# One core, packed attention and two feed-forward layers: loads over all partitions, a shared layout of e and v, other slots for raw weights, and a table that shifts the planner's order

## The chip, the cores and the metric

The kernel runs on one core of one Trainium2 chip. The metric is the device time of one launch in microseconds (us). A profile is one more execution, taken with the hardware profiler. Six queues matter: TensorE (PE; its weight loads are shown apart as PEld), VectorE (DVE), ScalarE (ACT), GpSimd (POOL), and the queue of SyncE (SP), which issues nearly all DMAs; ACT issues the others. Each engine takes its instructions strictly in program order and waits on semaphores for data from the others.

## The reference

```
p_packed = softmax(scale * p @ k.T) @ v              # per batch and head: 32 packed rows, 576 tokens, width 64
attn     = softmax(scale * q @ p_packed.T) @ p_packed
x = attn.transpose(0, 2, 1, 3).reshape(4608, 512)
h = x @ w_in                                          # 512 -> 1024
solu = h * softmax(h)
ln = (solu - mean(solu)) / sqrt(var(solu) + 1e-6) * g_ln
y = ln @ w_out                                        # 1024 -> 512
out = relu(y @ w2_in) ** 2 @ w2_out                   # 512 -> 2048 -> 512
```

There are 8 batches, 8 heads and 4608 = 8 x 576 tokens. The weights arrive as double-precision words, two 32-bit words for each value, and are put together on the engines.

## The kernel before

**Stages.** A batch's attention is done in two halves. `pack` computes p_packed: DVE transposes k (kT), q (qT) and p (pT) in blocks of 32 (L601, L637), PE makes the scores s (L615), DVE takes their maxima (mx), ACT their exponentials e, PE transposes e (pt, L680), ACT copies the result out (eT), PE multiplies it by v (ppp, L690), and DVE scales it into pp and pd (L694, L696). PE transposes those two (ptp) and ACT copies them out as ppf and ppq. `unpack` makes the second scores and their softmax (tiles a, m, d, aT), and G = p_packed @ w_in (pg, L626; ACT and DVE write it as a high part and a rest). Then h comes as aT times G, in 36 tiles of 128 tokens (`h_tile`): products ph, on DVE the maximum nm (L815) and the product e (L823), on ACT two passes, PE transposes (ptv), and ACT and DVE write the tile v (a high part by ACT and the rest by DVE, each in two pieces of 512 a tile). Two tiles make a y stage (`y_stage`): 96 products py (three for each pair of operands, since each operand is a high part and a rest), 18 such stages in all, written to y_dram. Beside that run the decodings of the weights: w_in (4 chunks of 1024 columns, `load_w_in`), w_out (4 chunks, `load_w_out`), and 16 pieces of w2_in (`prepare`, tiles w2raw, wx, wh), whose results go to z_dram and are loaded again (zi) for the last two stages: z (products px, pw, pz) and o (px, pa).

**The order.** No engine's order is written by hand. Each operation is recorded with an engine, an estimate of its time and an urgency. `Plan.order` plays the program through by these estimates: of the operations that are ready on an engine, the one with the least urgency goes first. `emit` repeats this with urgencies worked back from the end, keeps the best, and then records the instructions in the order found. A gate is a mark that holds back the first transposes (kT, qT) of a batch in this order until a given maximum nm is recorded; it puts no other wait on the chip than those two operations have anyway.

**Slots.** A tile waits until the tile that held its slot is done with. The raw words of w_out (wraw) sit in the two slots v00 and v01, where chunks 0 and 1 of w_in's raw words lie first. So the first two loads of w_out cannot be issued before chunks 0 and 1 of w_in are decoded, and SP, which issues in order, holds everything behind them back too. The raw tiles of k and q have three slots, those of v two.

**Decoding.** One chunk costs ACT one pass (L525) and DVE five; with `sign == DVE` two of DVE's put the sign in (L528, L529), with `sign == ACT` two ACT passes (L532, L534) take the place of the first of them. Before, w_in goes by DVE and w_out by ACT.

Of the kernel before, what the change touches and what calls it, by code (L numbers as in the profile page):

```python
# [94 lines left out]
class Plan:  # L95
# [241 lines left out]
    def emit(self, passes):  # L337
        order = self.order()
        best, kept = max(self.ends), None
        for _ in range(passes):  # L340
            self.backward()
            urgencies = [o.urgency for o in self.ops]
            order = self.order()
            if max(self.ends) < best:
                best, kept = max(self.ends), urgencies
        if kept:
            for o, u in zip(self.ops, kept):
                o.urgency = u
# [9 lines left out]
def kernel(  # L358
# [37 lines left out]
    ST = 256  # L396
    AB, RAW, TMP, VR, ET = 4, 3, 4, 2, 2
    LEAD = 2
    QA, GA, HA, TR, UN = 15.37, 149.84, 60.66, -52.41, -15.5
    WD, WDS, WIS = 101.7, 198.675, 19.564  # L400
    SIN, SOUT = DVE, ACT
    GX = 1
# [71 lines left out]

    RATES = {256: 205.0, 512: 303.0, 1024: 341.0, 1536: 372.0, 2304: 300.0, 3072: 378.0, 4096: 410.0, 8192: 400.0}
# [90 lines left out]
    def load_w_out(at, d):  # L566

        raw = wo_v.tile([P, C1 * P, 2], I32, "wraw", tag=f"v0{d % 2}")
        dma(-1995.0 + 0.1 * d, lambda: raw().rearrange("p (c d) w -> p c d w", c=C1),
            lambda: w_out_bits[:, 2 * d * P:2 * (d + 1) * P].rearrange("(c p) (d w) -> p c d w", p=P, w=2), P * C1 * P * 8, w=[raw], run=1024)  # L570
        x = wo_v.tile([P, C1 * P], F32, "wx", tag=f"v1{d % 2}")
        decode(at, raw, C1 * P, x, SOUT, add=(DVE,))
        xv = lambda: x().rearrange("p (c d) -> p c d", c=C1)

        def gain():
            for c in range(C1):
                nc.scalar.mul(xv()[:, c], xv()[:, c], g_neg[:, c:c + 1])
# [7 lines left out]
    KC, KJ = 3 * T, 2 * 3  # L585
# [42 lines left out]
    def pack(at, b):  # L628
# [10 lines left out]
        mx = [ab.tile([P, 2], F32, f"mx{g}") for g in range(NG)]  # L639
        e1s = [ab.tile([P, S], F32, "e1", bufs=2) for _ in range(NG)]  # L640
        s1 = []
# [5 lines left out]

        vs = []
        for g in range(NG):
            vr = ab.tile([P, HG, KJ, D], F32, "vr", bufs=VR)  # L650
            dma(first(b, "v", at + 1), lambda vr=vr: vr()[:KC].rearrange("p e j d -> p e (j d)"), lambda g=g: v[b, g::NG].rearrange(
                "e (p j) d -> p e (j d)", j=KJ), HG * S * D * 4, w=[vr], run=1536)
            vs.append(vr)

# [3 lines left out]
        for g in range(NG):  # L658
# [13 lines left out]

            eT = ab.tile([P, KJ, P], F32, "eT", bufs=ET)
            for hf in range(2):
                pte = bank("pt")
                js = range(hf * KJ // 2, (hf + 1) * KJ // 2)

                def pt_tr(js=js, pte=pte, e1=e1):
                    for n, j in enumerate(js):
                        nc.tensor.transpose(pte()[:KC, n * P:(n + 1) * P], e1()[:, j::KJ], ident)  # L680
                plan.op(PE, 3 * 109, at + 7, pt_tr, r=[e1], w=[pte], claim=[eT])
                hi_op(at + 7, 3 * P, lambda hf=hf, eT=eT: eT()[:KC, hf * 3:(hf + 1) * 3],
                      lambda pte=pte: pte()[:KC, :3 * P].rearrange("p (j n) -> p j n", n=P), [pte], [eT])

            ppp = bank("ppp")

            def pp_mm(g=g, ppp=ppp, eT=eT):
                for j in range(KJ):
                    for e in range(HG):
                        nc.tensor.matmul(ppp()[32 * e:32 * e + 32, :D], eT()[:KC, j, 32 * e:32 * e + 32], vs[g]()[:KC, e, j],  # L690
                                         start=j == 0, stop=j == KJ - 1)
            plan.op(PE, KJ * 2 * 80 + 60, at + 10, pp_mm, r=[eT, vs[g]], w=[ppp], claim=[pp, pd])
            plan.ops[-1].tiled = True
            plan.op(DVE, c_dve(D) + 60, at + 12, lambda g=g, ppp=ppp, rs=rs: nc.vector.tensor_scalar(  # L694
                pp()[:, g], ppp()[:, :D], rs(), None, op0=ALU.mult), r=[ppp, rs], w=[pp])
# [221 lines left out]
    for b in range(B):  # L917
# [354 lines left out]
```

## Time and profile before

| What | us |
|---|---|
| Three timed runs: median (lowest, highest) | 1243.34 (1242.59, 1245.89) |
| The profiled execution: its own time | 1245.66 |
| Its span, first to last instruction | 1243.9 |
| PE busy | 1174.1 (94%) |
| DVE busy | 886.0 (71%) |
| ACT busy | 793.0 (64%) |
| POOL busy | 167.8 (13%) |

The profiled execution took 1.8 us more than its span, and 2.3 us more than the median of the timed runs. A busy PE is not PE at its peak: products overlap in the array, so a matmul's duration is longer than the distance from its start to the next one's. Where the engine runs without a gap, that distance is what counts.

### The profile page before, as it was taken

The page shows a single profiled execution, that of the slowest core. Times are in us where ns is not written, and L with a number is a line of the kernel's source. Part 1 is how long each engine was busy: PE and PEld are TensorE (multiplying, and loading weights), DVE is VectorE, ACT ScalarE, POOL GpSimd, SP SyncE. Part 2 cuts the span into 40 slices and gives each one's busy share as a digit, 9 for nine tenths or more (in the row PEclk, how much of TensorE's full clock was granted, in tenths as well). Part 3 has the DMA queues.
Part 4 walks back from the last instruction along what each step waited for, and adds up shares of the span by engine and source line. Part 5 has one row for each costly group of instructions (what it writes and reads, how often), then busy time and mean ns, then how long its engine had stood idle before and what let it go on. Part 6 is the DMA issues. An engine that isn't in the chain of part 4 may idle for free.

```text
span 1243.9 us, 25577 instructions
## 1 busy us (share of the span) xinstructions
PE 1174.1 (94%) x9684; PEld 1088.7 (88%) x9684; DVE 886.0 (71%) x1724; ACT 793.0 (64%) x1669; POOL 167.8 (13%) x225
## 2 busy tenths in 40 slices
PE   3289999999999999889999999999999999999998
PEld 2036776788989899879999999999999999999998
DVE  4799988976476645437675857573779787878885
ACT  3388757766667766538787878786645454545452
POOL 0012543434244333000000000000000000000000
PEclk9989999999999999999999999999999999999999
DMA  9964988622322322995857565746994535262601
GB/s 259 196 157 118 226 203 218 167 65 93 112 69 77 115 77 72 367 363 182 263 189 257 191 234 191 233 153 219 382 399 153 165 103 164 92 189 67 191 14 52
DMA packets 174012, 218.75 MB, mean 176 GB/s; under 512 B 18240, under 2 KB 140608, under 8 KB 173120
## 3 DMA queue, kind: packets, MB, share of 16 engines
q1 hardware_dynamic: 133472, 192.20, 49.8%
q10 hardware_dynamic: 40416, 24.91, 6.6%
q8 instruction: 76, 1.25, 0.4%
q14 instruction: 48, 0.39, 0.1%
HBM read 131.08 MB, written 85.98 MB: 175 GB/s over the span
## 4 chain that ended last, share of the span: by engine, by line
PE 83%; DMA 7%; DVE 6%; ACT 2%; issue 1%; SPq 1%; ACTq 0%; DVEq 0%
PE px L510 10%; PE px L512 10%; PE px L511 10%; PE ph L808 7%; PE py L510 5%; PE pa L512 5%; PE pa L511 5%; PE pa L510 5%; PE py L512 5%; PE py L511 5%; PE pz L512 3%; PE pz L510 3%; PE pz L511 3%; PE s L615 2%; PE ptv L852 2%; DMA zi<-z_dram 1%
## 5 line engine op out<-in xcount | busy, mean ns | idle before, releaser
L492 ACT CAST cb<-ga 128x384 fp32r<-128x384 f32 x336 | 167.9, 514 | 161.5 <-PE pa L512 70.5
L495 DVE TENSOR_TENSOR cb<-ga,cb 128x384 fp32r<-128x384 f32 x336 | 180.8, 555 | 57.7 <-ACT cb L492 56.4
L510 PE MATMUL py<-v,wo 128*128 128x256 f32 x576 | 167.6, 291 | 2.9 <-ACT v L492 1.4
L511 PE MATMUL py<-v,wo 128*128 128x256 f32 x576 | 163.5, 284 | 0.8 <-DVE v L495 0.8
L512 PE MATMUL py<-v,wo 128*128 128x256 f32 x576 | 163.4, 284 | 0.0
L510 PE MATMUL px<-oi,cb 128*128 128x256 f32 x504 | 142.2, 282 | 0.8 <-ACT gw L1084 0.8
L512 PE MATMUL px<-oi,cb 128*128 128x256 f32 x504 | 142.3, 282 | 0.0
L510 PE MATMUL pa<-oi,cb 128*128 128x256 f32 x504 | 142.0, 282 | 0.0
L512 PE MATMUL pa<-oi,cb 128*128 128x256 f32 x504 | 142.0, 282 | 0.0
L511 PE MATMUL px<-oi,cb 128*128 128x256 f32 x504 | 142.0, 282 | 0.0
L511 PE MATMUL pa<-oi,cb 128*128 128x256 f32 x504 | 142.0, 282 | 0.0
L512 PE MATMUL px<-y,zi 128*128 128x384 f32 x384 | 129.7, 338 | 1.1 <-DMA zi<-z_dram 1.1
L510 PE MATMUL px<-y,zi 128*128 128x384 f32 x384 | 129.4, 337 | 1.3 <-ACT gw L1053 1.3
L511 PE MATMUL px<-y,zi 128*128 128x384 f32 x384 | 129.3, 337 | 0.0
L510 PEld LDWEIGHTS py<-v,wo 128*128 128x128 f32 x576 | 110.7, 192 | 10.6 <-issue 3.6
L511 PEld LDWEIGHTS py<-v,wo 128*128 128x128 f32 x576 | 110.7, 192 | 2.2 <-DVE v L495 1.2
L512 PEld LDWEIGHTS py<-v,wo 128*128 128x128 f32 x576 | 110.6, 192 | 0.0
L1057 DVE TENSOR_TENSOR gw<-pz,gw 128x384 f32<-128x384 f32 x96 | 53.3, 555 | 77.1 <-PE pz L512 58.0
L997 DVE TENSOR_TENSOR ga<-ga 128x384 f32<-128x384 f32 x192 | 100.5, 552 | 2.3 <-DMA ga<-g_dram 1.4
L510 PEld LDWEIGHTS px<-oi,cb 128*128 128x128 f32 x504 | 95.4, 189 | 1.0 <-ACT gw L1084 1.0
L512 PEld LDWEIGHTS px<-oi,cb 128*128 128x128 f32 x504 | 95.3, 189 | 0.1
L1065 ACT ACTIVATE gw<-gw 128x384 f32<-128x384 f32 x116 | 60.8, 524 | 54.3 <-DVE gw L1057 53.9
(142 smaller groups left out, 2941.1 us busy)
## 6 DMA issues: line engine op xcount, KB each, us to landing
g_dram<-gw SPq DMA_DIRECT2D x192, 192.0 KB, 2.6
ga<-g_dram SPq DMA_DIRECT2D x96, 384.0 KB, 4.1
zi<-z_dram SPq DMA_DIRECT2D x28, 512.0 KB, 8.7
oi<-o_dram SPq DMA_DIRECT2D x24, 512.0 KB, 9.5
kr<-in_k_dram SPq DMA_DIRECT2D x32, 288.0 KB, 5.5
qr<-in_q_dram SPq DMA_DIRECT2D x32, 288.0 KB, 6.1
vr<-in_v_dram SPq DMA_DIRECT2D x16, 576.0 KB, 7.4
y_dram<-ysb ACTq DMA_DIRECT2D x72, 128.0 KB, 2.0
```

The source lines that it names most:

```text
L492: plan.op(ACT, c_act(cols, sbuf=r[0].pool not in (psm, psh, pso)), at, lambda: nc.scalar.copy(out_(), in_()), r=r, w=w)
L495: plan.either(on(cols, *engines), at, lambda e: vec[e].tensor_tensor(out_(), in_(), hi_().bitcast(F32), op=ALU.subtract), r=r, w=w, port=i ...
L510: nc.tensor.matmul(ps, lh, rh, start=first, stop=False, skip_group_check=onto)
L511: nc.tensor.matmul(ps, lh, rl, start=False, stop=False, skip_group_check=onto)
L512: nc.tensor.matmul(ps, ll, rh, start=False, stop=last, skip_group_check=onto)
L615: nc.tensor.matmul(banks[u]()[32 * e:32 * e + 32, :SH].rearrange("p (m t) -> p m t", t=T), lhs(ps, e, f), ts[e // 2]()[ps, e % 2, :, f], s ...
L808: nc.tensor.matmul(ph()[:, fs], al[l]()[:, g], g_tiles[b, g]()[:, r, fs], start=ends[0] and g == 0 and t == 0, stop=ends[1] and g == NG - ...
L852: nc.tensor.transpose(pt()[:, c * P:(c + 1) * P], e()[:, (4 * t + c) * P:(4 * t + c + 1) * P], ident)
L997: plan.op(DVE, c_dve(cols), at, lambda: nc.vector.tensor_tensor(out_(), in0(), in1(), op=op), r=r, w=w, port=True)
L1057: plan.op(DVE, c_dve(HN), when(p, SN), lambda: nc.vector.tensor_tensor(t(), ps()[:, :HN], t(), op=ALU.add), r=[t, ps], w=[t])
L1065: nc.scalar.activation(t(), t(), AF.Relu)
```

## The change

It has seven parts.

1. q and k of a batch come in two loads of 128 partitions each instead of four of 64.
2. v comes in two loads over 128 partitions (heads in two groups of 64 partitions), in one slot instead of two. e is kept in a layout [partition, m, u, t], the one in which k already stands, so that PE can transpose it in pieces of 64 tokens by ordinary products with the identity, into the upper and lower half of the same PSUM bank: 18 products a batch in place of 12 transposes. The products with v then use 64 rows and 32 columns of the array: 72 a batch, all in one operation for both halves of the heads, in place of 2 x 24 with 96 rows.
3. The raw words of w_out go to the slots of batch 1's G (G10, G11), and the decoded words wx to v11 and w2raw.
4. w_in's sign goes to ACT as well (`SIN = ACT`).
5. The gate that held batch 2 back is now there for the batches 2 to 7, each on a later tile's maximum.
6. The planner counts 380 bytes per ns instead of 300 for runs of 2304 bytes.
7. A table NUDGES adds offsets to the urgencies of 128 ranges of operations after the planner's passes and before the last ordering.

```diff
+NUDGES = (
+    (464, 792, DVE, 0.87), (1690, 1955, DMA, 15.84), (690, 696, PE, 1.65), (705, 723, DVE, -8.52), (626, 748, DVE, 1.2),
...
@@ Plan.emit
+        for i0, i1, engine, later in NUDGES:
+            for o in self.ops[i0:i1]:
+                if engine is None or next(iter(o.engines)) == engine:
+                    o.urgency += later
         order = self.order()
@@ tile_packed_attention_moe_kernel
-    AB, RAW, TMP, VR, ET = 4, 3, 4, 2, 2
+    AB, RAW, TMP, VR, ET = 4, 3, 4, 1, 1
...
-    SIN, SOUT = DVE, ACT
+    SIN, SOUT = ACT, ACT
@@ load_w_out
-        raw = wo_v.tile([P, C1 * P, 2], I32, "wraw", tag=f"v0{d % 2}")
+        raw = m1.tile([P, C1 * P, 2], I32, "wraw", tag=f"G1{d % 2}")
...
-        x = wo_v.tile([P, C1 * P], F32, "wx", tag=f"v1{d % 2}")
+        x = wo_v.tile([P, C1 * P], F32, "wx", tag="v11") if d % 2 else m1.tile([P, C1 * P], F32, "wx", tag="w2raw")
@@ load_turned
+    def rows(x, b, h, n):
+        return x[b, h:h + NG * n].rearrange("(e g) (p m) d -> (g p) e (m d)", g=NG, m=HB)
...
-            for g in range(NG):
-                h0 = 2 * NG * eh + g
-                dma(first(b, name, at), lambda g=g, raw=raw: raw()[64 * g:64 * g + 64].rearrange("p e m f i -> p e (m f i)"), lambda h0=h0: x[b, h0:h0 + NG + 1:NG].rearrange(
-                    "e (p m) d -> p e (m d)", m=HB), 64 * 2 * HB * D * 4, w=[raw], run=2304)
+            dma(first(b, name, at), lambda raw=raw: raw().rearrange("p e m f i -> p e (m f i)"), lambda eh=eh: rows(x, b, 4 * eh, 2),
+                P * 2 * HB * D * 4, w=[raw], run=2304)
@@ pack
+        vr = ab.tile([P, HG, HB, D], F32, "vr", bufs=VR)
+        for eh in range(2):
+            dma(first(b, "v", at + 1), lambda eh=eh: vr()[:, 2 * eh:2 * eh + 2].rearrange("p e m d -> p e (m d)"), lambda eh=eh: rows(v, b, 4 * eh, 2),
+                P * 2 * HB * D * 4, w=[vr], run=2304)
...
-                    for n, j in enumerate(js):
-                        nc.tensor.transpose(pte()[:KC, n * P:(n + 1) * P], e1()[:, j::KJ], ident)
...
+                for i, m in enumerate(ms):
+                    for g in range(NG):
+                        nc.tensor.matmul(pte()[64 * g:64 * g + 64, i * P:(i + 1) * P], e1s[g]()[:, m].rearrange("p u t -> p (u t)"), ident, start=True, stop=True)
...
+            for m in range(HB):
+                for g in range(NG):
                     for e in range(HG):
+                        ps = slice(64 * g, 64 * g + 64)
+                        nc.tensor.matmul(ppp[g]()[32 * e:32 * e + 32, :D], eT()[ps, m, 32 * e:32 * e + 32], vr()[ps, e, m], start=m == 0, stop=m == HB - 1)
...
-            if b == 1:
-                gate(b + 1, [h_marks[int(b * S / P) - LEAD]])
+            if 1 <= b:
+                gate(b + 1, [h_marks[int(b * S / P) - 1 - b]])
```

What the table and the planner made of it, at three places. First ACT at the start of the program, from the last chunk of w_in (wi) to the first copies of G; wx and wraw are the words of w_out, in the second listing wraw is also those of w_in. Before:

```order
L525 ACTIVATE wi_327<-wraw 128x1024
L525 ACTIVATE wx<-wraw 128x1024
L532 ACTIVATE wraw<-wraw,tiny 128x1024
L534 ACTIVATE wraw<-wraw,mbig 128x1024
L525 ACTIVATE wx<-wraw 128x1024
L532 ACTIVATE wraw<-wraw,tiny 128x1024
L492 COPY ppq<-ptp 128x128
L492 COPY ppf<-ptp 128x256
L534 ACTIVATE wraw<-wraw,mbig 128x1024
L492 COPY G<-pg 128x512 x2
```

And now:

```order
L559 ACTIVATE wi_352<-wraw 128x1024
L568 ACTIVATE wraw<-wraw,mbig 128x1024
L566 ACTIVATE wraw<-wraw,tiny 128x1024
L559 ACTIVATE wx<-wraw 128x1024
L568 ACTIVATE wraw<-wraw,mbig 128x1024
L566 ACTIVATE wraw<-wraw,tiny 128x1024
L526 COPY ppf<-ptp 128x256
L526 COPY ppq<-ptp 128x128
L568 ACTIVATE wraw<-wraw,mbig 128x1024
L559 ACTIVATE wx<-wraw 128x1024
L566 ACTIVATE wraw<-wraw,tiny 128x1024
L526 COPY G<-pg 128x512 x2
```

Before, the copies ppq and ppf stood behind the first passes over both of w_out's first chunks (two rows wx<-wraw); now they stand behind that of the first chunk alone.

Second, DVE behind the maximum nm of the sixth h tile. Before, 32 instructions stand between it and the seventh tile's; the first eleven are:

```order
L815 TENSOR_REDUCE nm<-ph 128x1
L660 TENSOR_SCALAR nmx_1447<-mx_1411 128x1
L835 TENSOR_TENSOR den<-den,vs 128x1
L601 STREAM_TRANSPOSE qT<-qr 128x1152
L669 TENSOR_SCALAR rs_1464<-sm_1425 128x1
L838 SCALAR_TENSOR_TENSOR nb<-nmu,rst 128x1
L671 RECIPROCAL rs_1464<-rs_1464 128x1
L747 TENSOR_REDUCE d_1485<-a_1341 128x18
L601 STREAM_TRANSPOSE qT<-qr 128x1152
L749 TENSOR_SCALAR d_1485<-d_1485 128x18
L741 TENSOR_REDUCE m_1_1510<-a_1347 128x18
L669 TENSOR_SCALAR rs_1524<-sm_1458 128x1
```

Now the seventh tile's maximum is the last row of these:

```order
L854 TENSOR_REDUCE nm<-ph 128x1
L529 TENSOR_TENSOR v_1438<-ptv,v_1424 128x4x128
L874 TENSOR_TENSOR den<-den,vs 128x1
L786 TENSOR_REDUCE d_1500<-a_1395 128x18
L877 SCALAR_TENSOR_TENSOR nb<-nmu,rst 128x1
L862 SCALAR_TENSOR_TENSOR e,nmu<-ph,e 128x1024
L529 TENSOR_TENSOR v_1438<-ptv,v_1424 128x4x128
L788 TENSOR_SCALAR d_1500<-d_1500 128x18
L789 RECIPROCAL d_1500<-d_1500 128x18
L854 TENSOR_REDUCE nm<-ph 128x1
```

The transposes and the softmax of later batches (qT, kT, mx, rs) have moved behind the following tiles.

Third, SP's queue where the z stage begins: the last write of a prepared weight (z_dram<-wx), the loads of the first block of y (yr), and those of the prepared weights (zi). Before:

```order
L479 DMA z_dram_86<-wx 128x7x128
L479 DMA yr<-y_dram_79 128x2x768 x2
L479 DMA zi_6518<-z_dram_85 128x1024
L479 DMA zi_6525<-z_dram_85 128x1024
L479 DMA zi_6545<-z_dram_86 128x1024
```

And now:

```order
L513 DMA z_dram_86<-wx 128x7x128
L513 DMA zi_6606<-z_dram_85 128x1024
L513 DMA zi_6625<-z_dram_85 128x1024
L513 DMA zi_6642<-z_dram_86 128x1024
L513 DMA zi_6649<-z_dram_86 128x1024
L513 DMA zi_6674<-z_dram_85 128x1024
L513 DMA zi_6690<-z_dram_86 128x1024
L513 DMA yr<-y_dram_79 128x2x768 x2
```

Six loads of weights have moved ahead of the two of y.

## Rows read from the trace of the kernel before

**Rows 1.** Windows: length, PE, PEld, DVE, ACT, POOL busy (x instructions), PE clock, DMA share, GB/s
```profile
0.00:173.40 173.40, 119.80 (x1555) 78.09 (x1556) 144.40 (x254) 109.47 (x230) 37.02 (x53) 0.96 0.79 191
173.40:200.00 26.60, 22.77 (x328) 15.49 (x327) 22.43 (x50) 16.38 (x37) 13.75 (x17) 1.00 0.84 200
200.00:480.00 280.00, 280.00 (x2501) 248.62 (x2499) 183.13 (x332) 193.41 (x401) 110.47 (x149) 1.00 0.37 107
480.00:580.00 100.00, 92.05 (x579) 87.56 (x578) 48.24 (x90) 54.82 (x114) 6.58 (x7) 1.00 0.77 279
```

**Rows 2.** Timeline of DVE: first maximum nm, and the last piece of v ahead of the third y stage
```profile
81.90 1.30 DVE L815 TENSOR_REDUCE nm<-ph 128x1 f32<-128x1024 f32 x1
...
172.78 0.69 DVE L495 TENSOR_TENSOR v<-ptv,v 128x512 fp32r<-128x512 f32 x1
```

**Rows 3.** Timeline of DVE at the start; in brackets the idle time before
```profile
18.41 0.82 DVE L645 TENSOR_REDUCE mx<-s 128x1 f32<-128x288 f32 x2 [0.94 <-PE s L615]
...
42.11 0.35 DVE L696 TENSOR_SCALAR pd<-ppp,rs 128x128 f32<-128x128 f32 x1
44.30 1.38 DVE L601 STREAM_TRANSPOSE kT<-kr 128x1152 f32<-128x1152 f32 x1 [1.85 <-DMA kr<-in_k_dram]
51.93 1.38 DVE L601 STREAM_TRANSPOSE kT<-kr 128x1152 f32<-128x1152 f32 x1 [6.25 <-DMA vr<-in_v_dram]
```

**Rows 4.** Timeline of ACT at the start
```profile
40.77 1.15 ACT L525 ACTIVATE wx<-wraw 128x1024 f32<-128x1024 f32 x1 [5.22 <-DMA wraw<-in_moe_w_out_dram]
...
51.18 1.12 ACT L525 ACTIVATE wx<-wraw 128x1024 f32<-128x1024 f32 x1 [6.66 <-DMA wraw<-in_moe_w_out_dram]
...
53.46 0.24 ACT L492 COPY ppq<-ptp 128x128 f32<-128x128 f32 x1
...
55.75 1.07 ACT L492 COPY G<-pg 128x512 f32<-128x512 f32 x2 [0.61 <-PE pg L626]
```

**Rows 5.** Waits of PE, 480 to 580 us: engine, line, waited for, us, times, longest
```profile
PE pz L512 <- DMA zi<-z_dram: 2.8, 4, 0.9
...
PE px L512 <- DMA zi<-z_dram: 1.1, 2, 0.6
```

**Rows 6.** Groups of DVE by line: busy us, mean ns of one, idle before
```profile
L601 DVE STREAM_TRANSPOSE kT<-kr 128x1152 f32<-128x1152 f32 x16 | 21.9, 1371 | 13.5 <-DMA kr<-in_k_dram 7.2 <-DMA vr<-in_v_dram 6.2
...
L645 DVE TENSOR_REDUCE mx<-s 128x1 f32<-128x288 f32 x32 | 13.7, 448 | 2.5 <-PE s L615 2.3
...
L536 DVE SCALAR_TENSOR_TENSOR wx<-wx,wraw 128x1024 int32<-128x1024 int32 x4 | 5.1, 1270 | 0.0
L529 DVE SCALAR_TENSOR_TENSOR wi<-wraw,wi 128x1024 int32<-128x1024 int32 x4 | 4.9, 1221 | 0.0
...
L528 DVE TENSOR_SCALAR wi<-wi 128x1024 int32<-128x1024 int32 x4 | 2.8, 690 | 1.1 <-ACT wi L525 1.1
```

**Rows 7.** Chain of work, 240 to 275 us: start, length, what
```profile
246.96 1.02 PE pg L626 x16
...
251.51 1.40 PE ph L808 x6
...
259.41 0.12 PE py L512
...
260.61 0.98 PE pt L680 x9
...
263.46 0.81 PE ppp L690 x48
...
265.90 1.13 PE s L615 x32
```

**Rows 8.** Groups of ACT by line
```profile
L532 ACT ACTIVATE wraw<-wraw,tiny 128x1024 f32<-128x1024 f32 x4 | 5.6, 1399 | 0.1
L534 ACT ACTIVATE wraw<-wraw,mbig 128x1024 int32<-128x1024 f32 x4 | 5.2, 1304 | 0.1
```

**Rows 9.** Timeline of SP where z begins
```profile
502.48 31.74 SPq L479 DMA_DIRECT2D zi<-z_dram  x26
```

More of the change, by code (lines that the diff above doesn't have):

```diff
@@ L473, in c_pool @@
         return 150 + 2.1 * cols
-    RATES = {256: 205.0, 512: 303.0, 1024: 341.0, 1536: 372.0, 2304: 300.0, 3072: 378.0, 4096: 410.0, 8192: 400.0}
+    RATES = {256: 205.0, 512: 303.0, 1024: 341.0, 1536: 372.0, 2304: 380.0, 3072: 378.0, 4096: 410.0, 8192: 400.0}
     def dma(at, out_, in_, nbytes, r=(), w=(), spare=1500, queue=nc.sync, run=3072):
@@ L584 @@
     HB = NB // 2
-    KC, KJ = 3 * T, 2 * 3
     QUART = 8 * 15 + 2 * (2 * 0.4219 * SH + 3)
@@ L639, in pack @@
         mx = [ab.tile([P, 2], F32, f"mx{g}") for g in range(NG)]
-        e1s = [ab.tile([P, S], F32, "e1", bufs=2) for _ in range(NG)]
+        e1s = [ab.tile([P, HB, 2, T], F32, "e1", bufs=2) for _ in range(NG)]
+        rss = []
         s1 = []
@@ L646, in pack @@
                     out=mx[g]()[:, u:u + 1], in_=s1[g][u]()[:, :SH], axis=AX.X, op=ALU.max), r=[s1[g][u]], w=[mx[g]])
[L648 to L653, printed above, removed]
+        vr = ab.tile([P, HG, HB, D], F32, "vr", bufs=VR)
+        for eh in range(2):
+            dma(first(b, "v", at + 1), lambda eh=eh: vr()[:, 2 * eh:2 * eh + 2].rearrange("p e m d -> p e (m d)"), lambda eh=eh: rows(v, b, 4 * eh, 2),
+                P * 2 * HB * D * 4, w=[vr], run=2304)
         pp = ab.tile([P, NG, D], F32, "pp")
@@ L665, in pack @@
                 plan.op(ACT, c_act(SH, 2), at + 6, lambda u=u, g=g, e1=e1, nmx=nmx, sm=sm: nc.scalar.activation(
-                    e1()[:, u * SH:(u + 1) * SH].rearrange("p (t m) -> p m t", m=HB), s1[g][u]()[:, :SH].rearrange("p (m t) -> p m t", t=T), AF.Exp, bias=nmx(), scale=scale,
+                    e1()[:, :, u], s1[g][u]()[:, :SH].rearrange("p (m t) -> p m t", t=T), AF.Exp, bias=nmx(), scale=scale,
                     accum_out=sm()[:, u:u + 1]), r=[s1[g][u], nmx], w=[e1, sm])
@@ L671, in pack @@
             plan.op(DVE, 90, at + 7, lambda rs=rs: nc.vector.reciprocal(rs(), rs()), r=[rs], w=[rs])
[L673 to L678, printed above, removed]
-                    for n, j in enumerate(js):
-                        nc.tensor.transpose(pte()[:KC, n * P:(n + 1) * P], e1()[:, j::KJ], ident)
-                plan.op(PE, 3 * 109, at + 7, pt_tr, r=[e1], w=[pte], claim=[eT])
-                hi_op(at + 7, 3 * P, lambda hf=hf, eT=eT: eT()[:KC, hf * 3:(hf + 1) * 3],
-                      lambda pte=pte: pte()[:KC, :3 * P].rearrange("p (j n) -> p j n", n=P), [pte], [eT])
@@ L685, in pack @@
-            ppp = bank("ppp")
-            def pp_mm(g=g, ppp=ppp, eT=eT):
-                for j in range(KJ):
-                    for e in range(HG):
[L690 to L695, printed above, removed]
@@ L696, in pack, with pt_tr @@
-            plan.op(DVE, c_dve(2 * D) + 60, at + 12, lambda g=g, ppp=ppp, rs=rs: nc.vector.tensor_scalar(
-                pd()[:, :, g], ppp()[:, :D].rearrange("p (f i) -> p f i", f=2).unsqueeze(2).to_broadcast([P, 2, 2, T]), rs(), None, op0=ALU.mult), r=[ppp, rs], w=[pd])
+            rss.append(rs)
+        eT = ab.tile([P, HB, P], F32, "eT", bufs=ET)
+        for n in range(3):
+            pte = bank("pt")
+            ms = range(3 * n, 3 * n + 3)
+            def pt_tr(ms=ms, pte=pte):
+                for i, m in enumerate(ms):
+                    for g in range(NG):
+                        nc.tensor.matmul(pte()[64 * g:64 * g + 64, i * P:(i + 1) * P], e1s[g]()[:, m].rearrange("p u t -> p (u t)"), ident, start=True, stop=True)
+            plan.op(PE, 3 * 220, at + 7, pt_tr, r=e1s, w=[pte], claim=[eT])
+            plan.ops[-1].tiled = True
+            hi_op(at + 7, 3 * P, lambda n=n: eT()[:, 3 * n:3 * n + 3], lambda pte=pte: pte()[:, :3 * P].rearrange("p (m n) -> p m n", n=P), [pte], [eT])
@@ new lines, in pack, with pp_mm @@
+        ppp = [bank("ppp") for _ in range(NG)]
+        def pp_mm():
+            for m in range(HB):
+                for g in range(NG):
+                    for e in range(HG):
+                        ps = slice(64 * g, 64 * g + 64)
+                        nc.tensor.matmul(ppp[g]()[32 * e:32 * e + 32, :D], eT()[ps, m, 32 * e:32 * e + 32], vr()[ps, e, m], start=m == 0, stop=m == HB - 1)
+        plan.op(PE, HB * (2 * 0.4219 * D + 6) + 110, at + 10, pp_mm, r=[eT, vr], w=ppp, claim=[pp, pd])
@@ new lines, in pack @@
+        plan.ops[-1].tiled = True
+        for g in range(NG):
+            plan.op(DVE, c_dve(D) + 60, at + 12, lambda g=g: nc.vector.tensor_scalar(
+                pp()[:, g], ppp[g]()[:, :D], rss[g](), None, op0=ALU.mult), r=[ppp[g], rss[g]], w=[pp])
+            plan.op(DVE, c_dve(2 * D) + 60, at + 12, lambda g=g: nc.vector.tensor_scalar(
+                pd()[:, :, g], ppp[g]()[:, :D].rearrange("p (f i) -> p f i", f=2).unsqueeze(2).to_broadcast([P, 2, 2, T]), rss[g](), None, op0=ALU.mult),
+                r=[ppp[g], rss[g]], w=[pd])
```

26 lines of the change are left out of this document (added).

## Prediction

> **What bounds the kernel now.** I began with the busy time by stretch [rows 1]. Between 200 and 480 us TensorE (PE) is busy for 280.00 of 280.00 us; from 480 to 580, where the y stages end and z begins, for 92.05 of 100. Up to 173.40 it is busy for 119.80 us, and that flatters it: its matmuls there start far apart. VectorE (DVE) is busy for 144.40 of those 173.40 us. So the kernel is bound by PE, except in its first 173 us, which DVE sets, and for 8 us at the change to z. The reader should look for what moves the start of full PE work, and for nothing that only relieves DVE or ScalarE (ACT) after 200 us.
>
> The timeline of DVE dates that start [rows 2]: the first maximum nm comes at 81.90, and the last piece of v ahead of the third y stage ends at 172.78 + 0.69 = 173.5. From the third stage on the stages follow one another at PE's pace.
>
> What holds DVE up is seen at the start [rows 3, 4]. Of its 173.4 - 144.4 = 29.0 us of idle time, 1.85 + 6.25 = 8.1 us are waits of kT for batch 1's k and for a load queued near it; SP issues those loads behind the loads of w_out, which wait in order for the decoding of w_in. ACT stands in order too: it waits 5.22 us and then 6.66 us for w_out's raw words, and only then copies ppq (53.46), although pd was done at 42.46. G follows at 55.75, and nm 26.15 us after it.
>
> **The change, part by part.** The sum is made against the profiled execution, 1245.66 us; the median of the timed runs is 2.3 us lower.
>
> *The ramp.* The order of the change, walked through with the durations of the old trace, shows what DVE has ahead of the last v of the third y stage. 3 kT and 2 qT fewer (1.371 each, the same shape): -6.9. 6 mx: -2.7 [rows 6]. Four pieces a, one aT, m and d: -4.7; four pp and pd: -2.4, these by their rows in the same view. w_in's sign on ACT takes away two operations a chunk and adds one, (0.690 + 1.221 - 1.270) x 4: -2.5 [rows 6]. One e more: +1.2. That makes -18.0, and 126.4 us in place of 144.4. Its idle time was 29.0; without the 8.1 us, which go because the first two loads of w_out no longer wait for a decoding, it is 20.9. The stage then starts at 126.4 + 20.9 = 147.3, against 173.4: 26.1 us earlier. But not all of that is gained, since PE has done less by then. By PE's prices in the chain [rows 7], ahead of that stage stand 96 score products fewer (1.13/16 each, two rows a product: -6.8), 6 ptp fewer (0.109: -0.7), 6 ph more (1.40/6: +1.4), 60 transposes (0.109: 6.5) replaced by 27 pairs of new pieces at 0.255 (6.9; see below: +0.4), and 240 products ppp (0.81/24: 8.1) replaced by 27 steps at 0.135 (3.6: -4.5). That is -10.2. Gain: 26.1 - 10.2 = 15.9 us. The bounds: if DVE's idle time stays 29, the gain is 7.8; if the 11.0 us by which ppq stands behind pd also come off DVE's idle time, leaving 9.9, it is 26.9. I take the value between, since the row names the cause of the 8.1 us, while DVE was mostly at other work during the 11.0.
>
> Between 173.40 and 200 PE is still idle for 26.60 - 22.77 = 3.8 us [rows 1], on DVE and ACT work of the next batches. With this work put off I count it as gained: -3.8 (bounds 0 and -8, the latter if the half-filled stretches around those waits fill as well).
>
> *The transposes of e and the products with v.* No row shows a transposing product of 64 columns. The nearest is pg: eight products side by side on parts of the array, over 512 columns, take 1.02 [rows 7], so 128 columns take 0.255. A pair of pieces, one for each half of the PSUM bank, is 0.255 if the halves run side by side; nine pairs a batch make 2.3 us where twelve transposes took 1.31. The products with v: six steps of four columns took 0.81, or 0.135 each; nine steps with both halves beside each other make 1.22 where two groups took 1.62. Net +1.0 - 0.4 = +0.6 a batch, for 8 batches +4.6. Below: a pair costs one old transpose, 0.109: -0.7 a batch, -6. Above: nothing overlaps, +3.5 a batch, +28, of which the three batches in the ramp (10.5) are hidden behind DVE: +17.5 beyond my figure.
>
> The Trainium skill, on its page "TensorEngine Tiling (Array Packing)", section "Restrictions and Gotchas", speaks against this part: column tiling excludes the transposing mode for fp32 input, so the new pieces cannot have the price of the old ones. The trace has no piece of that form, so it cannot bear this out. At the old row's 0.109 a piece the part would come to 9 x 0.218 - 1.31 - 0.4 = +0.25 a batch, +2 in all; by the rule it stays at +4.6.
>
> *The change to z.* PE waits there 2.8 + 1.1 = 3.9 us for zi [rows 5], whose loads SP issues from 502.48 on [rows 9]. They follow the last prepared weight, and that follows one ACT cast. In the new order nine copies of py results stand behind that cast where seven stood; a copy comes with 24 products of 0.12 [rows 7], so the cast is 2 x 2.9 = 5.8 us earlier against the end of y, and six zi loads now stand ahead of y's own. I take the 3.9 us as gained: -4 (bounds 0 and -8, all the idle time of that stretch).
>
> *At nothing.* The bytes and issues of q, k and v: batch 0's first wait is for p, which is unchanged, and later loads lie behind the 280 us of full PE; with the cover gone each late kT costs what it waits, as the 6.25 did. One slot for v: the next v can only load after the products with the last, in the ramp one batch ahead of need. w_in's sign puts 4 x (1.399 + 1.304) = 10.8 us more on ACT [rows 8], in a stretch from 20 to 40 us where it is mostly idle; DVE's decoding steps need their results. Without that cover it is the second rival. wx in w2raw's slot: the first w2_in piece waits for w_out's last, with 280 us of PE work in front.
>
> *Sum.* 1245.66 - 15.9 - 3.8 + 4.6 - 4.0 = 1226.6; less 2.3: 1224 us.
>
> **Rivals.**
>
> *A larger gain.* With DVE's idle time at 9.9 and the transition wholly closed: -26.9 - 3.8 + 4.6 - 8 = -34, about 1209. For it: ppq stands behind one pass of w_out where it stood behind two. Against it: DVE was busy for most of those 11 us.
>
> *A smaller gain.* ACT's 10.8 us of sign passes stand ahead of ppf and G, so what the loads free is taken again: idle 29, transition -2: -7.8 - 2 + 4.6 - 2 = -7, about 1236. For it: batch 0's mx starts at 18.41 [rows 3], so there is little earlier work to cover the passes.
>
> *The halves don't overlap*, because they write one bank or load weights in turn: 1224 + 17.5 = 1242, no difference. Against it: products ppp, s and pg overlap side by side in all rows.
>
> *The gates come too late.* This is the case on the other side. A batch that waits for nm of an early tile has 7 to 11 tiles until its G is needed (the first tile of batch b+1 is number 4.5(b+1), the gate for it tile int(4.5b) - 1 - b). A y stage has 96 products of 0.12, 11.5 us, and its two tiles' ph and ptv come on top, so that seven tiles are at least 50 us. Batch 0's chain took 26 us from ppq to nm, and about 34 before that. If it takes more than the tiles' time when DVE and ACT are shared, PE waits at each batch. At 20 us for two batches: 1224 + 40 = 1264. For it: six batches are held where one was; against it: DVE is busy for only 183.13 of 280 us in that stretch [rows 1].
>
> **How the numbers follow.** Chances: forecast 0.60, its own range 1216 to 1232 (the bounds of each term taken half way); larger gain 0.13; smaller gain 0.13; no overlap 0.06; gates too late 0.08. The range of 8 in 10 takes in the larger gain down to 1208 and the smaller up to 1238; outside it are mainly the last two. A measurement of this kernel can tell about 0.3%, 3.7 us, from no change. Faster by more than that are the first three cases, 0.86; the same, no overlap and a margin, 0.07; slower, the gates, 0.07.
>
> **What would show it.** Right: ACT no longer waits ahead of ppq, which is copied soon after pd; the first nm near 63 (81.9 - 8.1 - 11.0); the third y stage begins near 148; kT of batch 1 waits for no load; nine pairs of new pieces take about 2.3 us in the chain and 72 ppp about 1.2; PE's waits for zi are gone. Wrong: a third stage at 155 or later; PE idle on kT, aT or G between 200 and 480 us; pieces at 0.4 us a pair or more; a wait for w2raw or vr that has taken the place of the one for wraw.

## The result, and the profile after

The changed kernel took 1224.95 us, the median of four runs (1223.1 to 1225.62); the kernel before, beside it, 1243.24. The ratio is 0.985, with a 95% interval of 0.983 to 0.987. The forecast was 1224. The profiled execution took 1225.62 us with a span of 1223.8, against 1245.66 and 1243.9.

The windows of the changed kernel, cut at the start of its third y stage (length, then busy time of PE, PEld, DVE, ACT and POOL, PE clock, DMA share, GB/s):

```profile
0.00:145.30 145.30, 109.19 (x1401) 70.97 (x1401) 128.35 (x213) 104.70 (x208) 35.79 (x52) 0.91 0.61 199
145.30:200.00 54.70, 54.70 (x865) 43.85 (x864) 44.76 (x95) 39.33 (x92) 20.27 (x28) 1.00 0.53 162
200.00:480.00 280.00, 279.30 (x2814) 246.50 (x2813) 183.24 (x339) 187.18 (x387) 113.15 (x148) 1.00 0.39 120
480.00:580.00 100.00, 95.50 (x580) 92.92 (x580) 54.72 (x110) 60.52 (x131) 0.00 (x0) 1.00 0.83 299
```

DVE was busy for 128.35 us ahead of the third y stage and idle for 17.0; before, it was 144.40 and 29.0 at 173.40 [rows 1]. PE has no idle time between 145.30 and 200.00, where it had 3.8 us behind 173.40. The clock that PE was granted ahead of the stage is lower than before, 0.91 against 0.96 [rows 1], so the earlier start of the stage does not come from the clock. The timeline of DVE in the changed kernel (start, length, line, operation, tiles, shapes; in brackets the idle time before it):

```profile
6.24 2.88 DVE L635 STREAM_TRANSPOSE kT<-kr 128x1152 f32<-128x1152 f32 x2 [6.24 <-DMA kr<-in_k_dram]
...
13.71 0.82 DVE L680 TENSOR_REDUCE mx<-s 128x1 f32<-128x288 f32 x2 [2.32 <-PE s L649]
...
21.78 1.23 DVE L570 SCALAR_TENSOR_TENSOR wi<-wi,wraw 128x1024 int32<-128x1024 int32 x1 [2.02 <-ACT wraw L568]
...
41.02 1.33 DVE L635 STREAM_TRANSPOSE kT<-kr 128x1152 f32<-128x1152 f32 x1
...
42.91 1.36 DVE L635 STREAM_TRANSPOSE kT<-kr 128x1152 f32<-128x1152 f32 x1
...
59.81 1.22 DVE L854 TENSOR_REDUCE nm<-ph 128x1 f32<-128x1024 f32 x1
...
144.52 0.68 DVE L529 TENSOR_TENSOR v<-ptv,v 128x512 fp32r<-128x512 f32 x1
```

Against [rows 2, 3]: the two kT of batch 1 wait for nothing, the first nm comes at 59.81 instead of 81.90, and the last v ahead of the third stage at 144.52 instead of 172.78. Not foreseen: DVE begins at 6.24, and with kT; before, its first instruction came at 12.28 and was pT:

```profile
12.28 0.45 DVE L637 STREAM_TRANSPOSE pT<-pr 128x256 f32<-128x256 f32 x1 [12.28 <-DMA pr<-in_p_dram]
```

The timeline of ACT shows ppq at 35.19 and G at 43.06; a pass over w_out's words still waits, but behind ppq and for DVE:

```profile
31.66 1.15 ACT L559 ACTIVATE wx<-wraw 128x1024 f32<-128x1024 f32 x1
...
35.19 0.27 ACT L526 COPY ppq<-ptp 128x128 f32<-128x128 f32 x1
...
40.73 1.16 ACT L559 ACTIVATE wx<-wraw 128x1024 f32<-128x1024 f32 x1 [4.10 <-DVE wi L578]
...
43.06 1.04 ACT L526 COPY G<-pg 128x512 f32<-128x512 f32 x2
```

The chain of work gives the new pieces their price: 36 rows of pt (18 products of one batch) take 2.12 us, where twelve transposes took 12 x 0.109 = 1.31 [rows 7].

```profile
154.92 2.12 PE pt L716 x36
157.04 1.58 PE ph L847 x6
158.62 1.59 PE ppp L728 x102
```

The products with v have 144 rows a batch, of which the chain shows only 102; from the first of them to the start of what follows they take 1.59 us, against 2 x 0.81.

**Where the time went.** To place the gain, I counted PE's lost time up to a point: the time there, less the PE work done by then, each instruction at the distance to the next where PE runs without a gap. The prices are those of [rows 7], the two new ones above, and from stretches of the same trace 0.119 for py and the products of o, 0.175 for those of z, 0.109 for ptv, and 0.43 for a row of ph while it is whole fp32. All PE work came to 1137.0 us before and 1143.2 after; the rest of the span is lost time. A stretch at a lower PE clock counts as lost time too. The same count for every run below, in us:

| Kernel | third y stage starts | lost by 200 | 200 to 480 | 480 to 580 | behind | ratio to before (95%) |
|---|---|---|---|---|---|---|
| before | 175.4 | 82.8 | 4.8 | 12.0 | 7.3 | 1 |
| changed | 145.3 | 57.2 | 7.4 | 7.5 | 8.5 | 0.985 (0.983 to 0.987) |
| changed, again (e9) | 145.0 | 56.8 | 7.3 | 6.6 | 8.4 | 0.981 (0.979 to 0.984) |
| e1 no table | 155.7 | 66.4 | 6.7 | 12.7 | 8.1 | 0.994 (0.992 to 0.996) |
| e2 old order, slots | 177.9 | 83.6 | 6.4 | 10.8 | 7.3 | 1.000 (0.998 to 1.001) |
| e3 old order, loads | 166.0 | 73.4 | 4.4 | 12.4 | 7.4 | 0.994 (0.991 to 0.996) |
| e4 old order, both | 167.2 | 77.9 | 4.5 | 12.6 | 7.3 | 0.994 (0.991 to 0.996) |
| e5 new order, 64-partition loads | 148.8 | 60.9 | 6.8 | 7.3 | 7.9 | 0.984 (0.982 to 0.987) |
| e6 new order, sign on DVE | 145.6 | 57.4 | 7.3 | 6.7 | 7.6 | 0.983 (0.980 to 0.985) |
| e7 new order, early DVE work | 155.4 | 67.3 | 6.4 | 7.6 | 8.0 | 0.991 (0.988 to 0.993) |
| e8 new order, late DVE work | 145.3 | 59.2 | 20.7 | 8.0 | 8.2 | 0.996 (0.995 to 0.998) |
| e10 old kernel, gates | 164.2 | 78.2 | 12.3 | 8.4 | 8.1 | 0.996 (0.994 to 0.998) |
| e11 no table, old gate | 184.1 | 72.5 | 5.7 | 2.2 | 7.3 | 0.989 (0.986 to 0.991) |
| e12 new order, y first | 146.8 | 58.7 | 7.3 | 16.0 | 9.4 | 0.990 (0.987 to 0.992) |

On the chips of the experiments the kernel before took 1243 to 1251 us, a wider spread than beside the changed kernel, so that kernels measured on different chips are compared by ratio, with some 0.3% to allow, or by this count. The count is that of one profiled execution each; those of e4 and e10 took 4.1 and 4.4 us more than the median of their runs, so that their lost time is too high by about as much. Before to changed: -25.6 by 200 us, +2.6, -4.5 and +1.2 behind it, and +6.2 of PE work: -20.1, the difference of the spans.

### The profile page after: what moved, and what is told of

Its sections match the earlier page's. It is cut to its first block, busy times and chain, and to the rows that moved or that the text cites. A ratio compares the mean times of both kernels' runs of the same rounds, so it can differ in the third digit from the quotient of the medians.

```text
span 1223.8 us, 26653 instructions
## 1 busy us (share of the span) xinstructions
PE 1177.2 (96%) x10260; PEld 1091.8 (89%) x10260; DVE 881.3 (72%) x1722; ACT 789.6 (65%) x1660; POOL 169.2 (14%) x227
## 3 DMA queue, kind: packets, MB, share of 16 engines
q8 instruction: 80, 1.31, 0.4%
## 4 chain that ended last, share of the span: by engine, by line
PE 85%; DVE 5%; ACT 4%; DMA 4%; issue 1%; POOL 0%; SPq 0%; ACTq 0%; DVEq 0%; POOLq 0%
PE px L544 10%; PE px L546 10%; PE px L545 10%; PE ph L847 7%; PE pa L544 5%; PE pa L546 5%; PE pa L545 5%; PE py L544 5%; PE py L546 4%; PE py L545 4%; PE s L649 3%; PE pz L544 2%; PE pz L546 2%; PE pz L545 2%; PE ptv L891 2%
## 5 line engine op out<-in xcount | busy, mean ns | idle before, releaser
L544 PEld LDWEIGHTS py<-v,wo 128*128 128x128 f32 x576 | 109.8, 191 | 10.6 <-issue 3.8
L544 PEld LDWEIGHTS px<-oi,cb 128*128 128x128 f32 x504 | 95.4, 189 | 1.0 <-ACT gw L1123 1.0
L546 PEld LDWEIGHTS px<-oi,cb 128*128 128x128 f32 x504 | 95.4, 189 | 0.9 <-DVE cb L529 0.9
L545 PEld LDWEIGHTS px<-oi,cb 128*128 128x128 f32 x504 | 95.4, 189 | 0.0
```

What stands on the lines that cost most here:

```text
L544: nc.tensor.matmul(ps, lh, rh, start=first, stop=False, skip_group_check=onto)
L545: nc.tensor.matmul(ps, lh, rl, start=False, stop=False, skip_group_check=onto)
L546: nc.tensor.matmul(ps, ll, rh, start=False, stop=last, skip_group_check=onto)
```

## The experiments

Where an order is kept, the list in which the planner recorded the operations was written into the kernel and read back, so that each engine has its rows in the same order.

**Which part carries the gain: the table, the slots, the loads (e1 to e4).** My theory was that of the prediction: the order puts DVE work off, and the slots end 8.1 us of waits. The rival: the loads.

e1, the changed kernel with `NUDGES = ()`.

> The changed kernel with an empty table of offsets; the planner orders it by itself, all other parts of the change stay. If the order is the larger part (18 us of DVE work put behind the third y stage), most of the gain is lost: 1235 to 1242 us, third y stage at 160 us or later. If loads and slots carry the gain, it stays within 3 us of the changed kernel: 1222 to 1228.

It took 1237.31 us, 0.994 of before. So with the new gates in place the table is worth 0.9 to 1.3% of the kernel before, more than half of the gain (e11 below sets this in proportion), but not in the way that was expected: DVE is busy for 128.1 us ahead of the third stage (155.7), so that the work ahead of it has shrunk without the table. What the table closes is lost time by 200 us (66.4 to 57.2) and at the change to z (12.7 to 7.5).

e2, the kernel before in its order, with

```diff
-        raw = wo_v.tile([P, C1 * P, 2], I32, "wraw", tag=f"v0{d % 2}")
+        raw = m1.tile([P, C1 * P, 2], I32, "wraw", tag=f"G1{d}") if d < 2 else wo_v.tile([P, C1 * P, 2], I32, "wraw", tag=f"v0{d % 2}")
```

> The kernel before, its order on every engine kept row by row, with only the raw words of w_out's chunks 0 and 1 in the slots of batch 1's G. If SP's wait for the decoding costs DVE 8.1 us of idle time that goes straight to the end: 1234 to 1237 us, kT of batch 1 without waits. If that wait is covered by other late things (ACT's passes over the same words, in the same order): 1241 to 1245, no change.

It took 1.000 of before. The waits did not go. The group of kT in this run (busy, mean ns, idle before) stands against the same group in [rows 6], with 13.5 us of idle time:

```profile
L601 DVE STREAM_TRANSPOSE kT<-kr 128x1152 f32<-128x1152 f32 x16 | 21.9, 1372 | 12.8 <-DMA kr<-in_k_dram 12.7
```

The queue of SP shows why. Of e2 first (start, length of the issue, what), then of the kernel before:

```profile
21.52 0.38 SPq L479 DMA_DIRECT2D wraw<-in_moe_w_out_dram  x1
22.82 7.62 SPq L479 DMA_DIRECT2D kr<-in_k_dram  x2
...
36.01 0.39 SPq L479 DMA_DIRECT2D wraw<-in_moe_w_out_dram  x1
```

```profile
28.35 0.38 SPq L479 DMA_DIRECT2D wraw<-in_moe_w_out_dram  x1
28.77 2.05 SPq L479 DMA_DIRECT2D kr<-in_k_dram  x2
...
35.71 0.39 SPq L479 DMA_DIRECT2D wraw<-in_moe_w_out_dram  x1
```

w_out's first load is issued 6.8 us earlier, without the wait for the decoding; but the two loads of k behind it then take 7.62 us to issue where they took 2.05, so that they are through at 30.4 and 30.8 us; the next load of w_out is no earlier. The wait for the decoding only stood in front of another. The loads already on their way are its likely cause: nothing on an engine released it, and from 21.5 to 30.5 us the DMA engines were busy throughout in both kernels (share 1.00 and 0.99, 363 and 366 GB/s).

e3, the kernel before in its order, with one DMA over 128 partitions for q and k where two of 64 were:

```diff
-                dma(first(b, name, at), lambda g=g, raw=raw: raw()[64 * g:64 * g + 64].rearrange("p e m f i -> p e (m f i)"), lambda h0=h0: x[b, h0:h0 + NG + 1:NG].rearrange(
-                    "e (p m) d -> p e (m d)", m=HB), 64 * 2 * HB * D * 4, w=[raw], run=2304)
+                plan.op(DMA, 430.0, first(b, name, at), lambda g=g, raw=raw, eh=eh: g or nc.sync.dma_start(out=raw().rearrange("p e m f i -> p e (m f i)"),
+                    in_=x[b, 4 * eh:4 * eh + 4].rearrange("(e g) (p m) d -> (g p) e (m d)", g=NG, m=HB)), w=[raw], lag=3700)
```

> The kernel before, its order kept, with q and k alone loaded over 128 partitions (one DMA where two were). By the prediction, which costed the shape of the loads at nothing: 1242 to 1245 us. If the loads bring the first kT forward (6.24 us in the changed kernel, 13.33 before) and the ramp with it: 1236 to 1239, with DVE's idle time ahead of the third y stage 5 us less.

It took 0.994 of before, and the third stage starts 9.4 us earlier with 20.4 us of idle time on DVE instead of 29.0. The idle time of kT is gone, though SP still issues w_out's loads behind the decoding (at 28.00 and 34.34):

```profile
L601 DVE STREAM_TRANSPOSE kT<-kr 128x1152 f32<-128x1152 f32 x16 | 21.6, 1358 | 0.0
```

The page's DMA issues say what the shape is worth (number, KB each, us from issue to landing), of before and of e3:

```profile
kr<-in_k_dram SPq DMA_DIRECT2D x32, 288.0 KB, 5.5
```

```profile
kr<-in_k_dram SPq DMA_DIRECT2D x16, 576.0 KB, 5.1
```

A load of twice the bytes over twice the partitions takes no longer. The Trainium skill bears on this with its page "SBUF — State Buffer", section "Door 1: The DMA port swizzle (why `[64,N]` ≈ `[32,N]`)": a transfer reaches only the ports that its partitions lie on, and the lower or the upper 64 partitions lie on half of them. On the same page of the Trainium skill, the section "Can I just issue two DMAs to hit both halves?" says that two transfers at once to the two halves do hardly better than one. These two rows, 5.5 and 5.1 us, and e3 agree.

e4, both edits at once.

> The kernel before, its order kept, with both edits of the two runs above. If the two gains are separate stretches of DVE's idle time they add up: 1229 to 1232 us if both exist, 1234 to 1237 if only that of the slots does, 1236 to 1239 if only that of the loads does.

0.994 again: the slots add nothing to the loads.

**Whether DVE still sets the time, and where (e5 to e8).**

e5, the changed kernel in its order, with two DMAs of 64 partitions again in each load of q and k:

```diff
-            dma(first(b, name, at), lambda raw=raw: raw().rearrange("p e m f i -> p e (m f i)"), lambda eh=eh: rows(x, b, 4 * eh, 2),
-                P * 2 * HB * D * 4, w=[raw], run=2304)
+            plan.op(DMA, 430.0, first(b, name, at), lambda raw=raw, eh=eh: [nc.sync.dma_start(out=raw()[64 * g:64 * g + 64].rearrange("p e m f i -> p e (m f i)"),
+                in_=x[b, 4 * eh + g:4 * eh + g + 3:NG].rearrange("e (p m) d -> p e (m d)", m=HB)) for g in range(NG)], w=[raw], lag=3700)
```

> The changed kernel, its order kept, with q and k again loaded in two DMAs of 64 partitions each instead of one of 128. If the loads carry 8 us of the gain in either order: 1231 to 1236 us. If the new order leaves enough time ahead of each load: within 3 us of the changed kernel, 1223 to 1228.

1227.67 us. By ratio no difference can be told; by the count, 3.7 us more are lost by 200, and e6, on the same chip, took 2.6 us less. The reverse edit was worth 9.4 us in the old order: what the loads bring depends on what waits for them. Here, with the loads of before, DVE begins at 7.01, the two kT of batch 1 wait for nothing, and DVE's idle time ahead of the third stage is 20.3 us (148.8 less 128.5 of work) instead of 17.0. So in the new order the waits for k are gone without the new loads as well.

e6, the changed kernel in its order, with the sign of w_in on DVE:

```diff
+            by_dve = n == F1 and x in wi
-            plan.op(ACT, c_act(n, 1, sbuf=True), at, lambda: nc.scalar.activation(
+            plan.op(ACT, c_act(n, 1, sbuf=True), at, lambda: by_dve or nc.scalar.activation(
                 high().bitcast(F32), high().bitcast(F32), AF.Sign, bias=tiny), r=[raw], w=[raw], port=True)
-            plan.op(ACT, c_act(n, 1, sbuf=True), at, lambda: nc.scalar.activation(
+            plan.op(ACT, c_act(n, 1, sbuf=True), at, lambda: by_dve or nc.scalar.activation(
                 high(), high().bitcast(F32), AF.Identity, scale=2.0 ** 30, bias=mbig), r=[raw], w=[raw], port=True)
-            plan.op(DVE, c_dve(n), at, lambda: stt(
+            plan.op(DVE, c_dve(n), at, lambda: (ts(bits(), bits(), 3, None, op0=ALU.logical_shift_left), stt(
+                out=bits(), in0=high(), scalar=-(1 << 31), in1=bits(), op0=ALU.bitwise_and, op1=ALU.bitwise_or)) if by_dve else stt(
                 out=bits(), in0=bits(), scalar=3, in1=high(), op0=ALU.logical_shift_left, op1=ALU.bitwise_or), r=[raw, x], w=[x], port=True)
```

> The changed kernel, its order kept, with w_in's sign put in by two DVE operations a chunk as before, and the two ACT passes left out. If DVE sets the ramp: 4 x 0.64 = 2.6 us slower, 1226 to 1229. If ACT's twelve passes between 17 and 36 us are what the first G waits for: faster, 1218 to 1223.

1225.05 us, and 57.4 us lost by 200 against 56.8 to 57.2: no difference, at a PE clock of 0.88 ahead of the third stage against 0.91. DVE's busy time ahead of the third stage is 130.9 instead of 128.4, its idle time 14.7 instead of 17.0: what the sign costs on DVE, it had waited for ACT (2.02 us in the timeline above). Neither theory held: not all DVE work ahead of the third stage sets its start.

e7, with each transpose of k and q done twice for the batches 0 and 1:

```diff
-            plan.op(DVE, c_dve(2 * S), at + 6, lambda t=t, raw=raw: nc.vector.transpose(
-                out=t().rearrange("p e m f t -> p (e m f t)"), in_=raw().rearrange("p e m f i -> p (e m f i)")), r=[raw] + gates.get(b, []), w=[t])
+            plan.op(DVE, c_dve(2 * S), at + 6, lambda t=t, raw=raw: [nc.vector.transpose(
+                out=t().rearrange("p e m f t -> p (e m f t)"), in_=raw().rearrange("p e m f i -> p (e m f i)")) for _ in range(2 if b <= 1 else 1)], r=[raw] + gates.get(b, []), w=[t])
```

> The changed kernel, its order kept, with the eight transposes of k and q of the batches 0 and 1 done twice: 8 x 1.37 = 11 us more DVE work ahead of the third y stage, nothing else. If DVE sets the ramp, nearly all of it comes at the end: 1232 to 1236 us. If PE or the loads set it now: at most 4 us, 1224 to 1229.

1234.86 us. The third stage starts at 155.4, and the last v ahead of it comes 10.1 us later than in the changed kernel (154.62 against 144.52), for 11 us of added work:

```profile
154.62 0.68 DVE L529 TENSOR_TENSOR v<-ptv,v 128x512 fp32r<-128x512 f32 x1
```

The span is 10.2 us longer than that of e9 (1232.5 against 1222.3). So work added to DVE at the head of batch 0 and batch 1 comes to the end nearly in full: this part of DVE's queue sets the ramp.

e8, the same for the batches 4 to 7 (`b >= 4`).

> The changed kernel, its order kept, with the sixteen transposes of k and q of the batches 4 to 7 done twice: 16 x 1.37 = 22 us more DVE work behind the ramp. If PE alone sets the time there and the gates leave the batches enough room: 1223 to 1227 us. If the gated batches come just in time: 5 us slower or more, 1230 to 1245.

1241.89 us, the span 16.9 us longer than that of e9. That PE alone sets the time there fails. The windows of e8 from 200 to 300 and 300 to 400 us, and PE's waits between 200 and 400 (line, waited for, us, times, longest):

```profile
200.00:300.00 100.00, 93.86 (x980) 77.68 (x969) 82.21 (x140) 59.28 (x127) 38.47 (x52) 0.98 0.45 137
300.00:400.00 100.00, 96.98 (x1163) 86.54 (x1162) 67.72 (x127) 61.84 (x133) 39.91 (x50) 0.98 0.33 100
```

```profile
PE s L649 <- DVE v L529: 3.2, 1, 3.2
PE ptv L891 <- DVE v L529: 3.0, 1, 3.0
PE ptv L891 <- DVE G L529: 1.0, 1, 1.0
PE py L544 <- DVE v L529: 1.0, 1, 1.0
```

DVE is idle for 18 of the first 100 us, and yet PE waits for it: the added transposes stand ahead of the pieces of v and G on DVE's queue. The longest of these waits ends with the piece of v behind a doubled qT (DVE's timeline in e8):

```profile
233.53 2.78 DVE L635 STREAM_TRANSPOSE qT<-qr 128x1152 f32<-128x1152 f32 x2
236.24 0.65 DVE L529 TENSOR_TENSOR v<-ptv,v 128x512 fp32r<-128x512 f32 x1
```

In the changed kernel no PE wait stands in that stretch, and its PE clock there is 1.00; of the 13.4 us that e8 loses beyond e9 between 200 and 480, up to 4 can be the lower clock (an estimate from the 0.98 of both windows). How much room the old order had there was not tried.

**What the gates do (e9 to e11).** e9 is the changed kernel once more, as the measure for its neighbours.

> The changed kernel once more, every row as it was, to have it on the same chip as the runs beside it. 0.983 to 0.987 of the kernel before; the runs that kept its order are compared with it.

1224.25 us, 0.981 of before (0.979 to 0.984), just below what was expected, which the interval still touches.

e10, the kernel before with the new gates alone:

```diff
-            if b == 1:
-                gate(b + 1, [h_marks[int(b * S / P) - LEAD]])
+            if 1 <= b:
+                gate(b + 1, [h_marks[int(b * S / P) - 1 - b]])
```

> The kernel before with the gates of the batches 3 to 7 alone, ordered by the planner. The order then has 124.8 us of DVE work ahead of the third y stage where it had 144.6. If the gates are what puts that work off, and DVE sets the ramp: third y stage near 154 us and, with the PE work that is put off too, 8 to 12 us faster: 0.990 to 0.994 of the kernel before. If work put off is only done later at PE's cost, 0.998 to 1.002.

0.996 of before, between the two expectations. The third stage starts 11.2 us earlier, of which 4.6 are left by 200 us, and between 200 and 480 it loses 12.3 where 4.8 were lost; the profiled execution is one that took 4.4 us more than the median. Work put off was in part only paid later.

e11, the changed kernel with `NUDGES = ()` and the one gate of before, the reverse of the diff above.

> The changed kernel with an empty table and with the one gate of before, ordered by the planner: 157.1 us of DVE work ahead of the third y stage, against 126.9 with the gates and without the table. If the gates carry the gain that the run without the table had: third y stage at 175 us or later and 0.998 to 1.006 of the kernel before. If the loads carry it: 0.992 to 0.995 as without the table.

The third stage starts at 184.1, 28 us later than in e1, and the kernel is faster: 1232.77 us, 0.989, better than either expectation. So the start of the third stage tells little by itself: 20 us more PE work lie ahead of it, and 6.1 us of lost time by 200 is what the gates gained between e11 and e1. Then e1 lost 12.7 us at the change to z and e11 2.2. One wait in e1 is 6.6 us long there:

```profile
PE ptv L864 <- ACT e L852: 6.6, 1, 6.6
```

Part of that loss is the PE clock, granted at 0.97 between 480 and 580 us in e1 and at 1.00 in e11: at most some 3 us, by an estimate from that share. Without the table the gates cost more at that end than they brought. And without table and gates the rest of the change already is 1.1% faster than the kernel before, so that both together add 0.4 to 0.8%, less than the table alone seemed to bring in e1. The planner's order was new in each of these runs, so that this says what it made of the gates, not what they are worth in the order of the table.

**The change to z (e12).** The changed kernel in its order, but with y's first two loads moved in SP's queue to ahead of the first load of zi.

> The changed kernel, its order kept but for SP: the two loads of y's first block again ahead of the loads of zi. If those six places were worth PE's waits for zi: 1 to 4 us slower than the changed kernel on the same chip, with more than 1.9 us of waits for zi where z begins. If the loads are spread over 16 queues anyway and hide behind the last py: within 1 us.

1234.81 us, 10.6 more than e9 beside it, and more than either expectation; 9.4 us of that are lost between 480 and 580. SP's waits from 440 to 540 us, and PE's waits for zi from 470 to 580, of e12:

```profile
SPq L513 <- PE ptv L891: 12.9, 1, 12.9
```

```profile
PE px L546 <- DMA zi<-z_dram: 2.7, 2, 2.2
PE pw L546 <- DMA zi<-z_dram: 2.3, 1, 2.3
PE pz L546 <- DMA zi<-z_dram: 1.8, 2, 1.4
PE px L544 <- DMA zi<-z_dram: 1.2, 1, 1.2
```

SP holds the loads of y until a tile's slot is free, for 12.9 us, and the loads of zi stand behind them. PE waits 8.0 us for zi, where e9 waited 0.9; the rest of the 9.4 us can be the PE clock, granted at 0.97 between 480 and 580 us against 1.00 in e9. In the changed kernel six of the loads of zi go out ahead of those of y, from 473.03 on (start, length, what):

```profile
472.61 0.38 SPq L513 DMA_DIRECT2D z_dram<-wx  x1
473.03 5.42 SPq L513 DMA_DIRECT2D zi<-z_dram  x6
485.43 1.28 SPq L513 DMA_DIRECT2D yr<-y_dram  x2
486.76 25.37 SPq L513 DMA_DIRECT2D zi<-z_dram  x20
```

## Why the prediction was right, and where it was not

The time was right to 1 us, but by terms whose errors cancelled, which was luck; and the cause that the prediction gave for one of its largest terms does not hold in the old order, where it could be tried alone.

**The work ahead of the third y stage** was forecast as 18.0 us less for DVE, and was 16.0 (144.40 at 173.40 to 128.35 at 145.30); one maximum nm more, 1.2 us, is among what the walk through the order missed. This lies in the order that the gates make: DVE's busy time ahead of that stage is 128.1 in e1 and 131.4 in e10, with the gates, and 160.4 in e11 without them. Of the 18.0, 2.5 were to come from moving the sign to ACT; e6 shows that they bring nothing, since DVE then waits for ACT. PE work put off was forecast as 10.2, and 9.6 measured (99.5 to 89.9).

**The start of the stage** was misread: the last v ahead of it was done at 173.5, but in the kernel before the stage began at 175.4, behind other products of PE; now it begins 0.1 us after that v. This is 2.0 us that the prediction did not have.

**DVE's idle time** was the step that failed: "without the 8.1 us, which go because the first two loads of w_out no longer wait for a decoding". e2 took away that wait, and 12.7 us of waits for k stayed, 7.5 of them batch 1's. The prediction had the loads "at nothing"; in the old order e3 ends the waits with them alone. In the new order the cause stays open: e5 has the loads of before and the new slots, and batch 1's kT waits for nothing there. The prediction's reason for the loads, that batch 0's first wait is for p, failed too: DVE took kT first, at 6.24, and this is 6.0 us of the 12.0 by which the idle time fell (29.0 to 17.0). The 8.1 are gone as well, and some 2 us of other waits have come. e5 begins at 7.01, so that most of the 6.0 is the order's and not that of the new loads. With all this the term came to 75.9 - 55.4 = 20.5 us (lost time at the start of the third stage), against 15.9.

**Up to 200** the forecast was 3.8; 5.1 were gained (6.9 lost before, 1.8 now).

**The new pieces** were forecast at +4.6 and cost +6.2. A pair of pieces takes 2.12 / 9 = 0.235, not 0.255; the products with v were mis-sized: a step takes 1.59 / 9 = 0.177 and not 0.135, so that 72 products cost what 2 x 24 did. The bound above, where nothing overlaps, was summed wrongly: by the prediction's own prices it is 9 x 0.51 - 1.31 + 18 x 0.135 - 1.62 = +4.1 a batch and not +3.5, which moves that rival by some us and not the forecast. The rule of the Trainium skill (page "TensorEngine Tiling (Array Packing)", section "Restrictions and Gotchas") that column tiling excludes the transposing mode for fp32 input is neither borne out nor refuted by this: 0.235 lies between 2 x 0.109 and 0.255.

**The change to z** was forecast at -4 and gave -4.5, but not as the prediction had it. Of PE's 3.9 us of waits for zi before, 1.9 stayed in the changed kernel (480 to 580 us):

```profile
PE pz L546 <- DMA zi<-z_dram: 1.9, 2, 1.4
```

So 2.0 of the 4.5 us are these waits (in e9 3.0 of 5.4), and the rest is other lost time of that stretch. e12 shows that the place of the six loads matters, 9.4 us in this order; that their gain comes through the earlier cast was argued, and was not tried.

**Not in the sum** were +2.6 us between 200 and 480 and +1.2 behind 580. The sum of the measured terms is -20.5 - 5.1 + 6.2 - 4.5 + 2.6 + 1.2 = -20.1, where -19.1 was forecast.

**ACT's passes** for the sign were rightly costed at nothing (e6). **The rival on the gates** did not come about, but e8 and e10 show that it is near: what is added to DVE behind 200 us comes out at three quarters. The shares of the table and of the gates cannot be parted further, since without the table the planner makes another order. Not tried by themselves were the shared layout of e and v with its loads (part 2), the slots of w_out in the new order (part 3), and the planner's rate (part 6).

## What to carry to other kernels

A wait names what came last, not all that held it up: before an edit that takes away the wait of a queue, ask whether the loads behind it could have landed sooner at all, and look at the bytes and the time of one load first. Count work at the bottleneck engine together with the start of a stage; a stage that begins 28 us later can belong to the faster kernel. What one part is worth depends on the others that are in place: the same loads brought 9.4 us in one order and 3 to 4 in another. An engine that is idle for a quarter of the time can still have no room, if what is added stands ahead of the work that the bottleneck needs next.

## What was not expected of the hardware

A load of 288 KB over 64 partitions took as long from issue to landing (5.5 us) as one of 576 KB over 128 (5.1). Two loads of k took 7.62 us to issue on SP when their turn came at 22.82 and 2.05 when it came at 28.77, so that they were through within 0.4 us of each other. Eight products of 64 rows by 32 columns, on two halves of the array at once, took 0.177 us; four of 96 rows took 0.135.
